# Low-rank token mixer after a Mamba-2 block: U's product as complete sums per channel tile, V's product as four 32-row matmuls

## The chip, the cores and the metric

The kernel runs on one core of a Trainium2 chip, everything in float32. The metric is the device time of one execution in microseconds (us). An execution under the profiler gives the profile that is quoted here.

## What is computed

Two stages follow each other. The first is a chunked state-space recurrence (Mamba-2) over 4 batches of 8 heads, 768 tokens, 32 channels per head; the second is a mixer over tokens of low rank and an MLP over channels. Cut to what matters for the change:

```python
def _moe_ref(x, U, V, w_ch1, w_ch2):          # x: (4, 768, 256), output of the first stage
    xt = x.transpose(0, 2, 1)                 # (4, 256, 768)
    h = xt @ U @ V                            # U: (768, 32), V: (32, 768)
    u = x + h.transpose(0, 2, 1)
    ch = np.maximum(u @ w_ch1, 0.0) @ w_ch2   # (256, 1024), (1024, 256)
    return (u + ch).astype(np.float32)
```

The weights U, V, w_ch1 and w_ch2 arrive as 64-bit floats and are made into 32-bit floats on the chip.

## The kernel before, in words

**Stages.** The program walks over 12 pairs of 128-token chunks (`pairs`, three for each batch). For pair k, `prep` scales B and C on VectorE and GpSimd, `turn` transposes them on TensorE (L298), `gram` multiplies them (L311, four groups of 32 rows, result in the PSUM tile `g` of four banks, masked into `M` by VectorE at L316), `state` carries the recurrence (L331, L345, L350), `ychannel` forms the output with channels on partitions (L368, L375, four groups of 32 columns; copied to `yT` by ScalarE at L378), and `ytokens` transposes it back (L386, copied to `ytok` by VectorE at L388).

**Mixer.** Once the three pairs of a batch are done, `mixer(b)` hands out its work in pieces that are spread between the steps of the next batch's pairs. `project` (L403) multiplies U with `ytok`: six matmuls, one for each token chunk, each giving 32 rows by 256 channels; chunk c goes to column group c % 4, so that the result holds four partial sums on 128 partitions, which ScalarE copies to `pT` (L405). Four pieces `mixed(k, n)` (L409) then multiply a 128-channel half of `pT` with `V4`, which holds V four times on 128 partitions: the product over 128 rows also adds up the four partial sums. VectorE adds the result to `uT` (L412). `up` (L419) is the first product of the MLP, with the relu on ScalarE (L424) or VectorE (L422), `down` (L431, L435) the second, copied out by ScalarE (L437).

**Weights.** `load_words` (L119) and the loop at L126 bring the 64-bit words into a ring of six buffers (`words`). `to_fp32` turns one buffer into 32-bit floats with five VectorE instructions (L237 `e`, L244 `top`, L241 `power`, L246 `top`, L248 `rest`), one on ScalarE (L240) and one on GpSimd (L250). There are eleven such pieces: U, V in two halves of 384 columns, four of w_ch1 and four of w_ch2. They are spread between the steps of the first batch.

**What sets the order.** The order on TensorE is the order of the program text, with the pieces dealt out by `some(n)` in the main loop: at a batch's end all that is left is issued, and then the first pieces of the new mixer. On the other engines and on the DMA queue (all loads are issued from SyncE, the row SP) a scheduler sets the order when the kernel is built. Each queue runs in that order, so that an instruction that waits holds up what is behind it.

Of the kernel before, what the change touches and what calls it, by code (L numbers as in the profile page):

```python
# [9 lines left out]
FP32 = mybir.dt.float32  # L10
# [5 lines left out]
ALU = mybir.AluOpType  # L16
# [4 lines left out]
def kernel(  # L21
# [27 lines left out]
    nc = tc.nc  # L49
    P = 128  # L50
    NB, NH, S, D = x.shape
    N = B.shape[-1]
    NC = S // P
    NPR = NC // 2
    DM = NH * D
    RK = moe_U.shape[1]
    DF = moe_w_ch1.shape[1]
    NM = DF // P
    NCB = DM // P
    HS = S // 2  # L60
    HT = HS // P
    Q = 32
    assert D == Q and 2 * N == Q and NH == 8 and RK == Q and NC % 2 == 0

    const = ctx.enter_context(tc.tile_pool(name="const", bufs=1))
    raw = ctx.enter_context(tc.tile_pool(name="raw", bufs=9))
    att = ctx.enter_context(tc.tile_pool(name="att", bufs=2))
    mix = ctx.enter_context(tc.tile_pool(name="mix", bufs=2))
# [5 lines left out]
    def bank(tag, *dims):  # L74
        return psum.tile([P, *dims], FP32, tag=tag, name=tag, bufs=BANKS[tag])
# [4 lines left out]
        out=a_sb,  # L80
        in_=a.rearrange("(g b) h (c s) -> g (b h c) s", g=2, s=P).rearrange(
            "g r s -> r g s"))
# [18 lines left out]


    U_sb = const.tile([P, NC, RK], FP32)
    V4 = const.tile([P, S], FP32)
    w1 = const.tile([P, NCB, DF], FP32)
    w2 = const.tile([P, NM, DM], FP32)
    weights = []
# [1 line left out]
    def words_of(dst):  # L109
        p, i, j = dst.shape  # L110
        t = raw.tile([P, 2 * WCOLS], INT32, tag="words", name="words", bufs=NWORDS)
        weights.append((dst, t[:p, :2 * i * j]))
        return t[:p, :2 * i * j]

    def load_words(dst, src):

        p, i, j = dst.shape
        t = words_of(dst)
        nc.sync.dma_start(out=t.rearrange("p (i j) -> p i j", i=i), in_=src)  # L119

    U2, V2, w12, w22 = (w.bitcast(INT32) for w in (moe_U, moe_V, moe_w_ch1, moe_w_ch2))
    load_words(U_sb, U2.rearrange("(c p) r -> p c r", p=P))
    for k in range(2):
        t = words_of(V4[:, None, ts(k, HS)])
        for g in range(4):
            nc.sync.dma_start(out=t[ts(g, RK)], in_=V2[:, ts(k, S)])  # L126
    for k in range(DF // WCOLS):
        for c in range(NCB):
            load_words(w1[:, c, None, ts(k, WCOLS)],
# [14 lines left out]
    def triangle(name, out, pattern, base, mult, in_=None):  # L144
# [9 lines left out]
           for v in range(2)]  # L154
# [7 lines left out]
                            op=ALU.subtract)  # L162
# [16 lines left out]
    for b in range(NB):  # L179
        g, o = divmod(b * NH * NC, R)  # L180
        nc.vector.tensor_scalar(
            out=la[:, b].rearrange("p c h -> p h c"),
            in0=la_ps[:, g, o:o + NH * NC].rearrange("p (h c) -> p h c", h=NH),
# [16 lines left out]
    for v in range(2):  # L200
# [14 lines left out]
        out=own, in0=d.rearrange("p b c (g r) -> p (b c g) r", r=4),  # L215
        in1=rmask[:, None, :].to_broadcast(own.shape), op=ALU.mult)
# [39 lines left out]
    for i in range(2):  # L256
        t = const.tile([P, 2 * NH, 2, N], FP32, name=f"bd{i}")
# [3 lines left out]
    yT, ytok = {}, {}  # L261
# [5 lines left out]
    def prep(k):  # L267
        b, q = pairs[k]
        bc = bc_sb.pop(k)
        s = st[k] = {}  # L270
        cs = slice(2 * q, 2 * q + 2)
        shape = [P, 2 * NH, 2, N]
        for i, (name, F, eng) in enumerate((("Bs", FB, nc.vector), ("Cs", FC, nc.gpsimd))):
            s[name] = t = att.tile(shape, FP32, tag=name, name=name)
            eng.tensor_tensor(  # L275
                out=t,
                in0=bc[:, i].rearrange("p c h n -> p (c h) n")[:, :, None, :].to_broadcast(shape),
                in1=F[:, b, cs].rearrange("p c h v -> p (c h) v")[:, :, :, None].to_broadcast(
                    shape),
                op=ALU.mult)  # L280
        s["bd"] = bd = bds[k % 2]
        n = 2 if q < NPR - 1 else 1
        sh = [P, n * NH, N]
        nc.gpsimd.tensor_tensor(
            out=bd[:, :n * NH, 0],
            in0=bc[:, 0, :n].rearrange("p c h n -> p (c h) n"),
            in1=FD[:, b, 2 * q:2 * q + n].rearrange("p c h -> p (c h)")[:, :, None].to_broadcast(
                sh),
            op=ALU.mult)

    def turn(k, c):

        s = st[k]
        tp = bank("w", 4, P)
        for i, name in enumerate(("Bs", "Cs")):
            flat = s[name].rearrange("p h v n -> p (h v n)")
            for g in range(2):
                nc.tensor.transpose(out=tp[:, 2 * i + g], in_=flat[:, ts(2 * c + g, P)],  # L298
                                    identity=ident)
        s["T", c] = T = att.tile([P, 4, P], FP32, tag="T", name="T", bufs=4)  # L300
        nc.scalar.copy(out=T, in_=tp)  # L301
# [91 lines left out]

    def mixer(b):
        uT = yT[b]
        pT = mix.tile([P, DM], FP32, tag="pT", name="pT")
        gT, hold = {}, {}

        def project():

            p = bank("w", DM)
            for c in range(NC):
                nc.tensor.matmul(out=p[ts(c % 4, Q)], lhsT=U_sb[:, c], rhs=ytok[b][:, c],  # L403
                                 start=(c < 4), stop=(c >= NC - 4), skip_group_check=True)
            nc.scalar.copy(out=pT, in_=p)  # L405

        def mixed(k, n):
            h = bank("w", HS)
            nc.tensor.matmul(out=h, lhsT=pT[:, ts(n, P)], rhs=V4[:, ts(k, HS)],  # L409
                             start=True, stop=True)  # L410
            u = uT[:, n, ts(k, HS)]
            nc.vector.tensor_tensor(out=u, in0=h, in1=u, op=ALU.add)  # L412

        def up(k, m):
            if m == 0:
                gT[k] = mix.tile([P, NM, HS], FP32, tag="gT", name="gT")
            g = bank("w", HS)
            for n in range(NCB):
                nc.tensor.matmul(out=g, lhsT=w1[:, n, ts(m, P)], rhs=uT[:, n, ts(k, HS)],  # L419
                                 start=(n == 0), stop=(n == NCB - 1))  # L420
            if m % 2:
                nc.vector.tensor_relu(gT[k][:, m], g)  # L422
            else:
                nc.scalar.activation(gT[k][:, m], g, AF.Relu)  # L424

        def down(k, j):
            if j == 0:
                hold[k] = mix.tile([P, HT, DM], FP32, tag="o", name="o")
            o = bank("w", DM)
            for n in range(NCB):  # L430
                nc.tensor.matmul(out=o[:, ts(n, P)], lhsT=uT[:, n, ts(HT * k + j, P)], rhs=ident,  # L431
                                 is_transpose=True, start=(n == 0), stop=False,
                                 skip_group_check=True)
            for m in range(NM):
                nc.tensor.matmul(out=o, lhsT=gT[k][:, m, ts(j, P)], rhs=w2[:, m],  # L435
                                 start=False, stop=(m == NM - 1), skip_group_check=True)
            nc.scalar.copy(out=hold[k][:, j], in_=o)  # L437
            if j == HT - 1:
                nc.sync.dma_start(
                    out=out[b, ts(k, HS)].rearrange("(j p) m -> p j m", p=P),  # L440
                    in_=hold[k])

        pieces = [project]
        for k in range(2):
            for n in range(NCB):
                pieces.append(lambda k=k, n=n: mixed(k, n))
        for k in range(2):
            for m in range(NM):
                pieces.append(lambda k=k, m=m: up(k, m))
            for j in range(HT):  # L450
                pieces.append(lambda k=k, j=j: down(k, j))
        return pieces


    with tc.manual_schedule(engines={PE}):
        last = len(pairs)
        prep(0)
        turn(0, 0)
        turn(0, 1)
        state(0)  # L460
        gram(0)
        prep(1)
        pieces = [lambda w=w: to_fp32(*w) for w in weights]
        for k in range(last + 1):
            b, q = divmod(k, NPR)

            def some(n):
                for _ in range(min(n, len(pieces))):
                    pieces.pop(0)()

            if k:
                ytokens(k - 1)
            if q == 0 and b:
                some(len(pieces))
                pieces = mixer(b - 1)
                some(5)
            if k == last:
                break
            quota = -(-len(pieces) // (NPR - q))
            parts = [quota // 3, quota // 3, quota - 2 * (quota // 3)]  # L480
            if k + 2 < last:
                prep(k + 2)
            if k + 1 < last:
                turn(k + 1, 0)
                some(parts[0])
                turn(k + 1, 1)
            else:
                some(parts[0])
            some(parts[1])
            ychannel(k)  # L490
            if k + 1 < last:
                state(k + 1)
                gram(k + 1)
            some(parts[2])
        some(len(pieces))
# [30 lines left out]
```

## Time and profile before

| what | us |
|---|---|
| median of 3 runs | 303.73 (302.91 to 304.68) |
| the profiled execution, its own time | 303.6 |
| its span, first to last instruction | 301.9 |
| busy in it: TensorE matmul (PE) | 258.4 |
| TensorE weight load (PEld) | 194.6 |
| VectorE (DVE) | 113.8 |
| ScalarE (ACT) | 58.5 |
| GpSimd (POOL) | 53.2 |

The profile's page gives busy time and idle time of each engine, a strip of 40 slices of the span, and the chain of waits that ended last. The trace behind it gives single instructions in order of time. A float32 matmul of the program appears as two matmul records there, so that a count of x8 is four matmuls of the program. SPq is the instruction queue of SyncE, from which the loads are issued.

### The profile page before, as it was taken

The numbers are of one execution on the slowest core, as the hardware profiler recorded it, in microseconds if no ns is written. First come the engines' busy times: TensorE is split into PE (matmuls) and PEld (weight loads), VectorE is DVE, ScalarE is ACT, GpSimd is POOL, SyncE is SP. The second block draws the span as 40 slices with busy tenths as digits, with TensorE's granted clock in tenths as the row PEclk, the third lists the DMA queues.
The fourth block names the chain that finished last, engine by engine and source line by source line (L and its number), as shares of the span: only waits on it lengthen the run. The fifth ranks groups of instructions, "written<-read, shape, count | busy, mean of one in ns | idle before, by whom it ended". The sixth has DMA issues, their size and how long they took to land.

```text
span 301.9 us, 4870 instructions
## 1 busy us (share of the span) xinstructions
PE 258.4 (86%) x2094; PEld 194.6 (64%) x2094; DVE 113.8 (38%) x201; ACT 58.5 (19%) x115; POOL 53.2 (18%) x69
## 2 busy tenths in 40 slices
PE   4549409019999999999999999999999999999994
PEld 4438307005768868857688688566886785587583
DVE  3249999994350154032500541325005103200200
ACT  5112213101221121013212220022121101111100
POOL 4343357461301103002102040001000000000000
PEclk9755967756999999999999999999999999999999
DMA  7989399899820100010001000100010001001001
GB/s 90 101 185 318 110 185 111 105 108 110 93 33 0 54 1 2 0 52 2 0 2 54 0 3 0 52 2 2 0 52 2 2 0 52 0 2 52 0 0 52
DMA packets 81141, 15.02 MB, mean 50 GB/s; under 512 B 76064, under 2 KB 79328, under 8 KB 81120
## 3 DMA queue, kind: packets, MB, share of 16 engines
q1 hardware_dynamic: 81120, 14.72, 27.5%
q8 instruction: 16, 0.26, 0.4%
q14 instruction: 5, 0.04, 0.0%
HBM read 11.57 MB, written 3.15 MB: 49 GB/s over the span
## 4 chain that ended last, share of the span: by engine, by line
PE 77%; DVE 10%; SPq 5%; DMA 3%; issue 1%; POOL 1%; ACT 1%; DVEq 0%; POOLq 0%
PE w L419 28%; PE w L435 27%; PE w L409 5%; PE y L375 4%; PE g L311 3%; PE y L368 3%; PE w L298 2%; SPq L93 2%; DVE M L316 2%; PE w L431 2%; DMA words<-in_moe_U_dram 2%; DVE rest L248 2%; SPq L94 2%; SPq L97 1%; DVE top L244 1%
## 5 line engine op out<-in xcount | busy, mean ns | idle before, releaser
L419 PE MATMUL w<-yT,w 128*128 128x384 f32 x256 | 86.9, 489 | 0.0
L435 PE MATMUL w<-w,gT 128*128 128x256 f32 x384 | 86.9, 379 | 0.0
L435 PEld LDWEIGHTS w<-w,gT 128*128 128x128 f32 x384 | 71.1, 190 | 8.7
L419 PEld LDWEIGHTS w<-yT,w 128*128 128x128 f32 x256 | 47.3, 190 | 29.3
L422 DVE TENSOR_SCALAR gT<-w 128x384 f32<-128x384 f32 x32 | 17.8, 557 | 64.0 <-PE w L419 64.0
L275 POOL TENSOR_TENSOR Cs<-bc,FC 128x512 f32<-128x512 f32 x12 | 16.4, 1364 | 78.5 <-issue 46.1
L316 DVE TENSOR_TENSOR M<-g,causal 128x1024 int32<-128x1024 int32 x24 | 28.3, 1217 | 3.1 <-PE g L311 3.0
L424 ACT ACTIVATE gT<-w 128x384 f32<-128x384 f32 x32 | 15.7, 491 | 55.3 <-PE w L419 55.3
L437 ACT COPY o<-w 128x256 f32<-128x256 f32 x24 | 8.9, 372 | 82.5 <-PE w L435 82.5
L301 ACT COPY T<-w 128x512 f32<-128x512 f32 x24 | 13.7, 585 | 36.8 <-PE w L298 36.4
L350 POOL TENSOR_TENSOR wide<-S,rmask 128x256 f32<-128x256 f32 x20 | 12.4, 633 | 47.4 <-DVE S L345 47.3
L388 DVE COPY ytok<-w 128x512 f32<-128x512 f32 x12 | 8.2, 683 | 31.4 <-PE w L386 31.4
L275 DVE TENSOR_TENSOR Bs<-bc,FB 128x512 f32<-128x512 f32 x12 | 10.8, 897 | 23.7 <-PE w L298 14.6
L345 DVE SCALAR_TENSOR_TENSOR S<-S,kept,w 128x32 f32<-128x32 f32 x32 | 6.3, 243 | 32.1 <-PE w L331 17.0
L375 PE MATMUL y<-M,x 128*32 128x128 f32 x384 | 14.4, 289 | 4.6 <-DVE M L316 4.6
L298 PE MATMUL w<-ident,Bs 128*128 128x128 f32 x48 | 10.6, 307 | 9.0 <-DVE Bs L275 9.0
L403 PE MATMUL w<-ytok,U_sb 128*32 128x256 f32 x48 | 5.5, 411 | 14.5 <-DVE ytok L388 14.5
L311 PE MATMUL g<-T 32*128 32x128 f32 x384 | 15.9, 308 | 0.0
L409 PE MATMUL w<-V,pT 128*128 128x384 f32 x32 | 13.9, 585 | 1.9 <-ACT pT L405 1.9
L298 PEld LDWEIGHTS w<-ident,Bs 128*128 128x128 f32 x48 | 7.1, 161 | 12.9 <-DVE Bs L275 9.0
L375 PEld LDWEIGHTS y<-M,x 128*32 128x32 f32 x384 | 10.2, 114 | 7.2 <-DVE M L316 5.9
L368 PEld LDWEIGHTS y<-T,wide 128*128 128x128 f32 x80 | 11.8, 212 | 4.3 <-POOL wide L350 1.9
(68 smaller groups left out, 195.3 us busy)
## 6 DMA issues: line engine op xcount, KB each, us to landing
words<-in_moe_w_ch_dram SPq DMA_DIRECT2D x8, 512.0 KB, 4.5
x<-in_x_dram SPq DMA_DIRECT2D x24, 128.0 KB, 3.8
out_dram<-o SPq DMA_DIRECT2D x8, 384.0 KB, 2.5
bc<-in_B_dram SPq DMA_DIRECT2D x24, 64.0 KB, 3.8
bc<-in_C_dram SPq DMA_DIRECT2D x24, 64.0 KB, 3.6
words<-in_moe_V_dram SPq DMA_DIRECT2D x8, 96.0 KB, 2.3
words<-in_moe_U_dram SPq DMA_DIRECT2D x1, 192.0 KB, 4.9
a_sb<-in_a_dram SPq DMA_DIRECT2D x1, 96.0 KB, 2.0
```

Of the source, the lines that this page charges most:

```text
L275: eng.tensor_tensor(out=t, in0=bc[:, i].rearrange("p c h n -> p (c h) n")[:, :, None, :].to_broadcast(shape), in1=F[:, b, cs].rearrange("p ...
L298: nc.tensor.transpose(out=tp[:, 2 * i + g], in_=flat[:, ts(2 * c + g, P)], identity=ident)
L301: nc.scalar.copy(out=T, in_=tp)
L311: nc.tensor.matmul(out=g_ps[:, r, c, g], lhsT=T[rows, g], rhs=T[rows, 2 + g], start=True, stop=True, skip_group_check=True)
L316: nc.vector.tensor_tensor(out=M[:, :, c].bitcast(INT32), in0=g_ps[:, :, c].bitcast(INT32), in1=causal[:, None, None, :].to_broadcast(sh), ...
L368: nc.tensor.matmul(out=y[:, c, g], lhsT=wide[:, g].rearrange("p r d -> p (r d)"), rhs=s["T", c][:, 2 + g], start=fresh, stop=False, skip_g ...
L375: nc.tensor.matmul(out=y[ts(r, Q), c, g], lhsT=x_sb[k][:, c, 4 * g + r], rhs=s["M"][:, r, c, g], start=False, stop=True, skip_group_check= ...
L409: nc.tensor.matmul(out=h, lhsT=pT[:, ts(n, P)], rhs=V4[:, ts(k, HS)], start=True, stop=True)
L419: nc.tensor.matmul(out=g, lhsT=w1[:, n, ts(m, P)], rhs=uT[:, n, ts(k, HS)], start=(n == 0), stop=(n == NCB - 1))
L422: nc.vector.tensor_relu(gT[k][:, m], g)
L424: nc.scalar.activation(gT[k][:, m], g, AF.Relu)
L435: nc.tensor.matmul(out=o, lhsT=gT[k][:, m, ts(j, P)], rhs=w2[:, m], start=False, stop=(m == NM - 1), skip_group_check=True)
```

## The change

`project` now issues 24 matmuls: for each of the six chunks four of 32 rows by 128 channels, one into each column group q. Group q multiplies channel tile q // 2, and a group's six matmuls accumulate, so that each group of 32 partitions of `pT` holds a complete sum (each channel tile twice). `V4` holds V's column half q % 2 in partition group q, half as wide as before. `mixed` is one piece: four matmuls over 32 rows each, in four row groups, into the four banks of the PSUM tile `g`; then the four additions in the order 0, 2, 1, 3. V is loaded with four transfers in place of eight and made into 32-bit floats by one `to_fp32` piece in place of two.

```diff
-    V4 = const.tile([P, S], FP32)
+    V4 = const.tile([P, HS], FP32)
...
-    for k in range(2):
-        t = words_of(V4[:, None, ts(k, HS)])
-        for g in range(4):
-            nc.sync.dma_start(out=t[ts(g, RK)], in_=V2[:, ts(k, S)])
+    t = words_of(V4[:, None])
+    for q in range(4):
+        nc.sync.dma_start(out=t[ts(q, RK)], in_=V2[:, ts(q % 2, S)])
...
-        pT = mix.tile([P, DM], FP32, tag="pT", name="pT")
+        pT = mix.tile([P, P], FP32, tag="pT", name="pT")
...
-            p = bank("w", DM)
+            p = bank("w", P)
             for c in range(NC):
-                nc.tensor.matmul(out=p[ts(c % 4, Q)], lhsT=U_sb[:, c], rhs=ytok[b][:, c],
-                                 start=(c < 4), stop=(c >= NC - 4), skip_group_check=True)
+                for q in range(4):
+                    nc.tensor.matmul(out=p[ts(q, Q)], lhsT=U_sb[:, c],
+                                     rhs=ytok[b][:, c, ts(q // 2, P)],
+                                     start=(c == 0), stop=(c == NC - 1), skip_group_check=True)
             nc.scalar.copy(out=pT, in_=p)
 
-        def mixed(k, n):
-            h = bank("w", HS)
-            nc.tensor.matmul(out=h, lhsT=pT[:, ts(n, P)], rhs=V4[:, ts(k, HS)],
-                             start=True, stop=True)
-            u = uT[:, n, ts(k, HS)]
-            nc.vector.tensor_tensor(out=u, in0=h, in1=u, op=ALU.add)
+        def mixed():
+
+            h = bank("g", 4, 4 * P)
+            for q in range(4):
+                rows = ts(q, Q)
+                nc.tensor.matmul(out=h[:, q, :HS], lhsT=pT[rows], rhs=V4[rows],
+                                 start=True, stop=True, skip_group_check=True)
+            for q in (0, 2, 1, 3):
+                u = uT[:, q // 2, ts(q % 2, HS)]
+                nc.vector.tensor_tensor(out=u, in0=h[:, q, :HS], in1=u, op=ALU.add)
...
-        pieces = [project]
-        for k in range(2):
-            for n in range(NCB):
-                pieces.append(lambda k=k, n=n: mixed(k, n))
+        pieces = [project, mixed]
...
-                some(5)
+                some(2)
```

On TensorE, at the end of each batch, the queue held this before (here the second batch; `L298` is `turn`, `L419` is `up`):

```order
L386 MATMUL w<-ident,yT 128x128 x4
L403 MATMUL w<-ytok,U_sb 32x256 x6
L409 MATMUL w<-V_97,pT 128x384 x4
L298 MATMUL w<-ident,Bs 128x128 x2
L298 MATMUL w<-ident,Cs 128x128 x2
L419 MATMUL w<-yT,w_98 128x384 x4
```

and holds this now, from `project` on, with the waits that the instructions carry:

```order
L403 MATMUL w<-ytok,U_sb 32x128 [waits Activation_49]
L403 MATMUL w<-ytok,U_sb 32x128 x15
L403 MATMUL w<-ytok,U_sb 32x128 [waits DVE_49]
L403 MATMUL w<-ytok,U_sb 32x128 x7
L413 MATMUL g<-V_97,pT 128x384 [waits Activation_49]
L413 MATMUL g<-V_97,pT 128x384 x3
L297 MATMUL w<-ident,Bs 128x128 [waits PE_49]
L297 MATMUL w<-ident,Bs 128x128
L297 MATMUL w<-ident,Cs 128x128 x2
L424 MATMUL w<-yT,w_98 128x384 [waits DVE_49] x2
```

The place is the same; `project` has four times as many matmuls, the four of V's product stand without a wait between them, and the first two matmuls of `up` (over the two channel tiles) each carry a wait of their own on VectorE.

On VectorE, while the weights are made into 32-bit floats, this stood before (128x384 are the halves of V, 128x512 is the first piece of w_ch1):

```order
L237 TENSOR_SCALAR e<-words 128x384
L244 TENSOR_SCALAR top<-words 128x384
L241 SCALAR_TENSOR_TENSOR power<-words,power 128x384
L237 TENSOR_SCALAR e<-words 128x512
L316 TENSOR_TENSOR M<-g,causal 128x4x256 x2
L246 TENSOR_TENSOR top<-top,power 128x384
L248 SCALAR_TENSOR_TENSOR rest<-words,power 128x384
L241 SCALAR_TENSOR_TENSOR power<-words,power 128x512
```

and now, from the first instruction of V on:

```order
L236 TENSOR_SCALAR e<-words 128x384
L243 TENSOR_SCALAR top<-words 128x384
L236 TENSOR_SCALAR e<-words 128x512
L243 TENSOR_SCALAR top<-words 128x512
L240 SCALAR_TENSOR_TENSOR power<-words,power 128x384
L344 SCALAR_TENSOR_TENSOR S<-S,kept,w 128x32
L245 TENSOR_TENSOR top<-top,power 128x384
L247 SCALAR_TENSOR_TENSOR rest<-words,power 128x384
```

The second half of V is gone (the rows before are those of that half), and two instructions of w_ch1's first piece have moved up between V's `top` and V's `power`.

On SyncE's queue the loads of weights and of the next pair (`bc`, `x`) stood so before:

```order
L119 DMA words<-in_moe_U_dram 128x6x64
L126 DMA words<-in_moe_V_dram 32x768 x8
L119 DMA words<-in_moe_w_ch_dram 128x1024 x4
L119 DMA words<-in_moe_w_ch_dram 128x2x512 x3
L93 DMA bc<-in_B_dram 128x8x16
```

and stand so now:

```order
L119 DMA words<-in_moe_U_dram 128x6x64
L125 DMA words<-in_moe_V_dram 32x768 x4
L119 DMA words<-in_moe_w_ch_dram 128x1024 x4
L119 DMA words<-in_moe_w_ch_dram 128x2x512 x2
L93 DMA bc<-in_B_dram 128x8x16
```

Four transfers of V fewer stand ahead of the next pair's loads, and one transfer of w_ch2 fewer, which now comes behind them.

## Rows read from the trace of the kernel before

**Rows 1.** The page: span, and the strip of 40 slices (tenths of each slice).
```profile
span 301.9 us, 4870 instructions
...
PE   4549409019999999999999999999999999999994
...
DVE  3249999994350154032500541325005103200200
...
PEclk9755967756999999999999999999999999999999
```
**Rows 2.** Windows: length, busy us (instructions) of PE, PEld, DVE, ACT, POOL; clock, DMA share, GB/s.
```profile
53.00:66.90 13.90, 0.10 (x4) 0.00 (x0) 13.90 (x22) 2.17 (x3) 8.31 (x7) 0.62 0.94 104
66.90:73.40 6.50, 5.95 (x12) 2.94 (x13) 4.10 (x8) 0.37 (x1) 1.26 (x1) 0.50 1.06 113
73.40:80.00 6.60, 6.60 (x28) 4.17 (x27) 1.81 (x4) 2.15 (x4) 1.54 (x1) 0.99 1.04 113
```
**Rows 3.** The chain that ended last, around the first batch's end: start, us, what.
```profile
66.33 0.61 DVE ytok L388
...
66.98 1.09 PE w L403 x4
...
68.52 5.31 PE w L409 x8
73.83 0.44 PE w L298 x4
74.26 1.94 PE w L419 x6
```
**Rows 4.** The timeline of VectorE, GpSimd and SP's queue while V is made into floats.
```profile
23.99 0.35 DVE L237 TENSOR_SCALAR e<-words 128x384 int32<-128x384 int32 x1
...
25.02 0.56 DVE L241 SCALAR_TENSOR_TENSOR power<-words,power 128x384 int32<-128x384 int32 x1 [0.41 <-ACT power L240]
...
27.28 0.90 DVE L237 TENSOR_SCALAR e<-words 128x384 int32<-128x384 int32 x1
...
29.67 0.41 DVE L237 TENSOR_SCALAR e<-words 128x512 int32<-128x512 int32 x1
...
32.27 0.54 DVE L246 TENSOR_TENSOR top<-top,power 128x384 int32<-128x384 int32 x1
...
33.21 0.68 DVE L241 SCALAR_TENSOR_TENSOR power<-words,power 128x512 int32<-128x512 int32 x1
33.81 1.22 DVE L244 TENSOR_SCALAR top<-words 128x512 int32<-128x512 int32 x1
...
33.36 1.38 POOL L250 TENSOR_TENSOR V<-rest,top 128x384 f32<-128x384 f32 x1 [4.03 <-DVE rest L248]
...
20.78 15.24 SPq L119 DMA_DIRECT2D words<-in_moe_w_ch_dram  x7
```
**Rows 5.** The timeline around the second batch's end, all engines.
```profile
130.25 0.64 PE L403 MATMUL w<-ytok,U_sb 128*32 128x256 f32 x8
...
131.77 0.37 ACT L405 COPY pT<-w 128x256 f32<-128x256 f32 x1 [1.48 <-PE w L403]
...
132.20 2.85 PE L409 MATMUL w<-V,pT 128*128 128x384 f32 x8 [0.47 <-ACT pT L405]
133.15 1.20 DVE L412 TENSOR_TENSOR yT<-w,yT 128x384 f32<-128x384 f32 x2 [2.10 <-PE w L409]
```
**Rows 6.** The same timeline, the products in column groups (L375) and row groups (L311).
```profile
141.46 1.08 PE L375 MATMUL y<-M,x 128*32 128x128 f32 x32
...
142.61 0.59 ACT L378 COPY yT<-y 128x512 f32<-128x512 f32 x1 [2.28 <-PE y L375]
142.76 1.17 PE L311 MATMUL g<-T 32*128 32x128 f32 x32
...
144.00 2.36 DVE L316 TENSOR_TENSOR M<-g,causal 128x1024 int32<-128x1024 int32 x2 [0.29 <-PE g L311]
```
**Rows 7.** The chain that ended last, at the last batch's end.
```profile
252.33 2.85 PE w L409 x8
```

## The prediction, made before the change had run

> **What bounds the kernel now.** I read the page's strip first. From about 75 us on TensorE is busy without a break and its granted clock is full; before that VectorE is the busy engine, TensorE mostly waits, and the clock is often near half [rows 1]. The kernel has two regimes, then: up to the first batch's end VectorE makes the weights into floats, after it TensorE streams the MLP. The windows show where one passes into the other: from 53.0 to 66.9 us VectorE is busy for all 13.90 us and TensorE for 0.10; from 66.9 to 73.4 TensorE is busy for 5.95 of 6.50 us, at a clock of 0.50, the lower level of 1.2 GHz; then the clock is full [rows 2]. The chain says the same in single steps: VectorE's copy of the last tokens at 66.33, U's product from 66.98, V's product from 68.52 for 5.31 us, `turn` for 0.44, and `up` from 74.26 [rows 3]. So three things can move the end: VectorE's work before 66.3, the steps between that copy and the first `up` of each of the four batches, and the time at which the clock rises.
>
> The sum is made against the profiled execution's own 303.6 us, which is 0.13 under the median of the runs, 303.73. About 0.5%, or 1.5 us, is what a measurement of this kernel can tell from no change.
>
> **The change part by part.**
>
> *One conversion fewer.* VectorE's five instructions for V's second half stood on the chain. From the start of its `e` at 27.28 to the next piece's `e` at 29.67 are 2.39 us, from its second `top` at 32.27 to the next piece's `power` at 33.21 are 0.94 us [rows 4]: 3.33 us. Some of it was not the instructions' own: undisturbed, `e` takes 0.35 and `power` 0.56 [rows 4], and two of the first length and three of the second make 2.4 us; the rest came while GpSimd worked beside them, and GpSimd's work for the first half stays. On the other side GpSimd's addition for the second half (33.36, 1.38 us) goes, beside which a `top` of w_ch1 took 1.22 us where `e` of the same shape takes 0.41 [rows 4]: 0.8 more. And the 0.41 us for which `power` waited for ScalarE [rows 4] is now filled by two instructions of w_ch1. The bounds are 2.0 us (the five overlap a little at their ends) and 4.5 us (3.33 + 0.8 + 0.41). I take 2.4 + 0.8, less the overlap: **3.1 us**. The work queued behind is VectorE's own, so the saving should reach the copy at 66.33. ScalarE's and GpSimd's instruction for that half go too; both had slack (2.17 and 8.31 us busy of 13.90, [rows 2]), and I give nothing for them.
>
> *Loads.* Four transfers fewer stand ahead of w_ch1, and the next pair's loads stand before a load of w_ch2 that waited for a free buffer: in the row of 15.24 us, seven issues of weights held up everything behind them [rows 4]. VectorE was busy anyway in that time, so earlier data brings nothing by itself: 0 us. What could cost is that VectorE now needs w_ch1's first piece two places after V; its load is issued four transfers earlier, which is my reason to expect no wait.
>
> *U's product, full clock (second to fourth batch).* It becomes 24 matmuls of 128 columns, six in each column group. The rate: `up` takes 1.94 us for three matmuls of 384 columns [rows 3], 0.647 each, 1.68 ns a column. The nearest rows are `ychannel`'s, 16 matmuls of the same shape in four column groups: from their start at 141.46 to ScalarE's copy at 142.61 are 1.15 us [rows 6], against 4 x 128 x 1.68 ns = 0.86 us of streaming in one group, so that 0.29 us is start and tail. Six in a group: 1.29 + 0.29 = 1.58 us. Sixteen of the 24 need only older tokens and run while VectorE copies the last ones. Before, U's product began at 130.25 and the copy to `pT` at 131.77 [rows 5]; now that copy would begin at 131.83. It has 128 columns: 256 take 0.37 us [rows 5] and 512 take 0.59 [rows 6], so about 0.26. V's product then begins at 132.15 (0.06 for the two signals), as before (132.20).
>
> *V's product, full clock.* Before: 2.85 us from 132.20, then `turn` for 0.44, so `up` began at 135.49 [rows 3, 5]. Now four matmuls run side by side. The nearest rows are `gram`'s: 16 matmuls over 32 rows in four row groups and four banks, 142.76 to VectorE's first mask at 144.00, 1.24 us, of which 0.86 is streaming [rows 6]. One matmul of 384 columns in each group streams 0.647, so the first addition can begin 1.03 us after the start, at 133.18. An addition takes about 0.56 (two in 1.20 with a wait between, [rows 5]); `turn` lies beside it. `up` begins with the tile that the first addition makes, at 133.8, and its second matmul wants the second addition, which is done before the first matmul's 0.647 us are over. Gain 1.7 us each at the second and third batch: **3.4 us**. At the fourth there is no `turn`: before, `up` began at 252.33 + 2.85 = 255.18 [rows 7]; now 1.6 us after a start at 252.3, at 253.9. Gain **1.2 us**. The other two additions run beside `up`; the banks of `g` are next wanted by `gram`, some ten us later.
>
> *A rule that speaks against it.* The rows of `gram` hold 0.38 us over streaming, with products of another shape on both sides [rows 6], and the sum has this once for each batch. The Trainium skill, "TensorEngine Tiling (Array Packing)", section Key Properties, says that a change of tiling mode drains the engine; the change adds one such switch for each batch. If the overhead of `gram`'s rows did not hold that drain, a second 0.38 us would come on top four times, and the sum would be 1.5 us later.
>
> *The first batch's end, at half clock.* The copy begins at 66.33 - 3.1 = 63.2, and TensorE goes on at 63.9 (66.98 less 3.1). Eight matmuls of U's product are left: 1.2 us at half clock, ScalarE's copy and signals 0.3, so V's product begins at 65.4. Its first addition begins 1.03 + 0.65 = 1.7 us later, at 67.1, and `up` could begin at 67.7; but `turn` behind V's product, 0.9 us at this clock, ends at 67.9. `up` begins at 67.9 instead of 74.26: 6.3 us earlier, of which 3.1 is the conversion.
>
> But at 74.26 the clock was full. It rose at 73.4 [rows 2], 4.9 us after V's product had begun and 6.4 us after TensorE had resumed. If it again rises 4.9 us after V's product begins, that is 70.3; from 67.9 to 70.3 `up` runs at half speed and loses 1.2 us. Bounds: no loss, if it rises as `up` begins; 3.2 us, if only the unbroken work counts and it takes the 6.4 us from there. I take 1.2, the row's own distance. Net **5.1 us**.
>
> Sum: 5.1 + 3.4 + 1.2 = 9.7; 303.6 - 9.7 = **293.9 us**.
>
> **The rivals.**
>
> *The conversion saves nothing.* VectorE then waits for data where V's second half was: for w_ch1's first piece, or for the next pair. For it: the DMA share is 0.94 to 1.06 around 66.9 us [rows 2]. Against it: VectorE never waited for those transfers before, and there are fewer bytes. The first `up` is then at 71.0; V's product begins at 68.5 as before, so the clock rises at 73.4 and 1.2 us are lost. The first batch's end brings 2.0 instead of 5.1: 297.0 us.
>
> *The additions become the bound.* `up` waits for all four. The Trainium skill, the same page, section PSUM Bottleneck, warns that tiling speeds up TensorE and not the emptying of PSUM. The mechanism here: V's product takes a quarter of the streaming time, and the additions keep their 0.56 us. If all four had to be done, `up` would begin about 1.5 us later at each batch: 1.5 x 3, and 1.1 at the first (partly at half clock), 5.6 in all: 299.5 us. Against it: the first two matmuls of `up` each have a wait of their own on VectorE.
>
> *The clock falls at the later batch ends.* TensorE now idles around 0.3 us for `pT` and 0.2 to 1 for the first addition. Each fall would cost half of a stretch as long as the 6.4 us above, 3.2 us, three times 9.6: 303.5 us, no change. Against it: before, it stood idle for 0.47 us at the same place [rows 5] and the strip stays at 9 [rows 1].
>
> *Slower: the column groups do not run side by side in U's product.* All four read the same tokens through separate weights. One after another, 24 matmuls of 0.215 us are 5.2 us instead of 1.58: 3.6 more at three batch ends, and 2.3 at the first, where eight are left at half clock; 13.1 in all, 307.0 us. It decides from about 4.0 us for the 24 on, where the loss is the gain. Against it: `ychannel`'s 16 take 1.08 us [rows 6], and eight records before, 0.64 us [rows 5], were four matmuls of 0.43 us each, already side by side.
>
> **How the numbers follow.** Forecast 0.78, first rival 0.10, additions 0.05, clock 0.04, column groups 0.03. Only the last two are not faster by over 0.5%; half a hundredth or so of the forecast goes there too. Faster 0.92, same 0.04, slower 0.04. The range: from 293.9 the conversion's upper bound takes 1.4 off and the clock's 1.2; both at once are unlikely, 291.6. Upwards the conversion's lower bound adds 1.1, the clock's 2.0, the second drain 1.5; the first rival lies at 297.0. Two of these at once, or the first rival with one, give about 298.2. Beyond it lie the last three rivals, 0.12, and a little of the forecast.
>
> **What would show it.** In the profile after: the copy to `ytok` before U's product near 63.2; TensorE's first `up` near 67.9 and the clock's rise near 70.3; U's product in 1.6 us and V's in about 1.0 at the later batches; `up` 1.6 us after V's product begins. The prediction is wrong if VectorE shows idle time on a DMA before 60 us, if `up` follows the fourth addition, or if the clock leaves its full level after 80 us.

## The result, and the profile after

| | before | changed |
|---|---|---|
| median, us | 303.83 (302.91 to 304.68, 4 runs) | 295.37 (294.73 to 296.49, 4 runs) |
| the profiled execution's own time, us | 303.6 | 296.49 |
| its span, us | 301.9 | 294.8 |

The ratio is 0.9726, with a 95% interval of 0.9683 to 0.9769: 2.7% faster, 1.5 us slower than the 293.9 us of the forecast and inside its range. The profiled execution of the changed kernel was the slowest of its four, so that its trace shows a gain of 7.1 us where the medians show 8.5.

The page of the changed kernel, the lines that answer to [rows 1]:

```profile
span 294.8 us, 5144 instructions
...
PE   4447631819999999999999999999999998999994
...
DVE  2339999794530244034401541325005103200100
...
PEclk9776955775999999999999999999999999999999
```

The two regimes are still there, VectorE first and TensorE after, and the clock never leaves its full level once it has risen. The first batch's end in the chain that ended last (start, us, what), for [rows 3]:

```profile
64.69 0.61 DVE ytok L387
...
65.35 1.13 PE w L403 x16
...
66.82 1.66 PE g L413 x8
68.48 1.05 PE w L297 x4
69.53 4.02 PE w L424 x8
```

The copy stands 1.64 us earlier than before, not 3.1. From there to the first `up` (L424) are 4.84 us, where it had been 7.93 and 4.7 were forecast. Eight records of `up` take 4.02 us, which is neither the 2.58 of the full clock nor twice that. The windows show why, for [rows 2]:

```profile
65.30:72.20 6.90, 6.47 (x33) 3.66 (x34) 4.35 (x8) 0.92 (x3) 1.27 (x1) 0.50 0.90 95
72.20:80.00 7.80, 7.80 (x118) 5.65 (x118) 2.98 (x8) 2.08 (x4) 3.11 (x4) 0.99 1.09 118
```

The clock stays at 0.50 (1.2 of 2.4 GHz) until 72.3, so `up` ran for 2.77 us at half speed, and its eight records took 1.44 us longer than 2.58 (1.2 forecast). At the second batch's end the timeline of all engines reads, for [rows 5]:

```profile
126.96 1.52 PE L403 MATMUL w<-ytok,U_sb 128*32 128x128 f32 x48
...
128.54 0.27 ACT L406 COPY pT<-w 128x128 f32<-128x128 f32 x1 [1.54 <-PE w L403]
...
128.86 0.93 PE L413 MATMUL g<-V,pT 32*128 32x384 f32 x8 [0.39 <-ACT pT L406]
...
129.92 1.95 DVE L417 TENSOR_TENSOR yT<-g,yT 128x384 f32<-128x384 f32 x4 [2.17 <-PE g L413]
...
130.54 0.30 PEld L424 LDWEIGHTS w<-yT,w 128*128 128x128 f32 x2 [0.40 <-DVE yT L417]
130.54 2.85 PE L424 MATMUL w<-yT,w 128*128 128x384 f32 x8 [0.17 <-DVE yT L417]
131.00 1.77 PEld L424 LDWEIGHTS w<-yT,w 128*128 128x128 f32 x6 [0.17 <-DVE yT L417]
```

U's product takes 1.58 us up to ScalarE's copy (1.58 forecast), V's product 1.06 up to the first addition (1.03), and `up` begins 1.68 us after V's product (1.65). But its first eight records take 2.85 us instead of 2.58. Three narrow windows of TensorE's timeline, each of which takes in one record more, show where the 0.27 us lie:

```profile
130.54 0.59 PE L424 MATMUL w<-yT,w 128*128 128x384 f32 x1 [0.17 <-DVE yT L417]
...
130.54 0.91 PE L424 MATMUL w<-yT,w 128*128 128x384 f32 x2 [0.17 <-DVE yT L417]
...
130.54 1.24 PE L424 MATMUL w<-yT,w 128*128 128x384 f32 x3 [0.17 <-DVE yT L417]
```

The first record takes 0.59 us, and each further one adds 0.32 or 0.33, as in an unbroken row of them (2.58 for eight). The third belongs to the second matmul; the load of its weights waited for the second addition and began at 131.00, but it came in time. So the 0.27 us are all the first record's: its weight load waits for the first addition together with the matmul and begins only at 130.54, where there is no matmul left in front to hide it. V's product of the kernel before took the same 2.85 for eight records of 384 columns, after one wait [rows 5]. That is 0.27 us at each of the three later batches; at the first, `turn` stands right in front of `up`.

### The profile page after: what moved, and what is told of

The parts are those of the page before. It is cut to its first block, busy times and chain, and to the rows that moved or that the text cites. A ratio compares the mean times of both kernels' runs of the same rounds, so it can differ in the third digit from the quotient of the medians.

```text
span 294.8 us, 5144 instructions
## 1 busy us (share of the span) xinstructions
PE 252.9 (86%) x2238; PEld 193.3 (66%) x2238; DVE 109.2 (37%) x196; ACT 57.1 (19%) x114; POOL 50.9 (17%) x68
## 4 chain that ended last, share of the span: by engine, by line
PE 77%; DVE 9%; SPq 7%; DMA 3%; issue 1%; POOL 1%; ACT 1%; DVEq 0%; POOLq 0%
PE w L424 29%; PE w L440 28%; PE y L374 4%; PE g L310 3%; PE y L367 3%; SPq L94 3%; SPq L93 2%; DVE M L315 2%; PE w L297 2%; DMA words<-in_moe_U_dram 2%; SPq L97 2%; PE w L436 2%; PE w L403 2%; DVE rest L247 2%; PE g L413 2%; DVE power L240 1%
## 5 line engine op out<-in xcount | busy, mean ns | idle before, releaser
L424 PE MATMUL w<-yT,w 128*128 128x384 f32 x256 | 88.7, 497 | 1.1 <-DVE yT L417 1.1
L424 PEld LDWEIGHTS w<-yT,w 128*128 128x128 f32 x256 | 48.0, 193 | 32.0 <-DVE yT L417 2.7
L274 POOL TENSOR_TENSOR Cs<-bc,FC 128x512 f32<-128x512 f32 x12 | 15.5, 1290 | 74.8 <-issue 44.7
L374 PE MATMUL y<-M,x 128*32 128x128 f32 x384 | 15.1, 300 | 6.7 <-DVE M L315 6.7
L367 PE MATMUL y<-T,wide 128*128 128x128 f32 x80 | 12.1, 294 | 7.4 <-POOL wide L349 7.2
L274 DVE TENSOR_TENSOR Bs<-bc,FB 128x512 f32<-128x512 f32 x12 | 9.3, 776 | 23.6 <-PE w L297 14.6
L249 POOL TENSOR_TENSOR w<-rest,top 128x512 f32<-128x512 f32 x8 | 12.1, 1508 | 16.0 <-DVE rest L247 15.4
L310 PEld LDWEIGHTS g<-T 32*128 32x128 f32 x384 | 13.6, 212 | 0.6
```

The costliest lines, as they stand in the source:

```text
L274: eng.tensor_tensor(out=t, in0=bc[:, i].rearrange("p c h n -> p (c h) n")[:, :, None, :].to_broadcast(shape), in1=F[:, b, cs].rearrange("p ...
L310: nc.tensor.matmul(out=g_ps[:, r, c, g], lhsT=T[rows, g], rhs=T[rows, 2 + g], start=True, stop=True, skip_group_check=True)
L367: nc.tensor.matmul(out=y[:, c, g], lhsT=wide[:, g].rearrange("p r d -> p (r d)"), rhs=s["T", c][:, 2 + g], start=fresh, stop=False, skip_g ...
L374: nc.tensor.matmul(out=y[ts(r, Q), c, g], lhsT=x_sb[k][:, c, 4 * g + r], rhs=s["M"][:, r, c, g], start=False, stop=True, skip_group_check= ...
```

## The experiments

They ran in two groups, each on one chip together with the kernel before. Its median was 304.1 us in the group of the repetition, the products, the conversion and the filler, and 303.99 in the group of the other four. The changed kernel's 295.82 us, which the others are held against, is of the first group.

### The changed kernel again

No edit.

> The changed kernel once more, unchanged, as the level that the others are compared with and for a second profile. Expected 295.4 us (294.7 to 296.5). What the second profile should settle: in the first one U's words landed 0.84 us later than before the change (20.48 against 19.64). If that comes from w_ch1's loads standing four transfers earlier, they land late again, near 20.4; if it is a thing of one execution, they land near 19.7 and the copy to ytok stands near 63.9 instead of 64.69.

Measured: 295.82 us (294.88 to 296.23), ratio 0.9741 (0.9694 to 0.9788). U's words did land earlier this time, by 1.19 us, but the copy stood at 64.30, only 0.39 earlier, since VectorE then waited in another place. Its timeline:

```profile
19.31 0.26 DVE L236 TENSOR_SCALAR e<-words 128x192 int32<-128x192 int32 x1 [2.99 <-DMA words<-in_moe_U_dram]
25.00 0.43 DVE L236 TENSOR_SCALAR e<-words 128x512 int32<-128x512 int32 x1 [0.74 <-DMA words<-in_moe_w_ch_dram]
55.81 0.43 DVE L243 TENSOR_SCALAR top<-words 128x512 int32<-128x512 int32 x1 [1.61 <-POOL w L249]
```

So the late landing of U is no property of the change: in ten profiled executions of these kernels VectorE began U's `e` between 18.98 and 20.50 us. The second row is the wait that the first rival named, for w_ch1's first piece, 0.74 us long, in one execution of the eight that have that order. It is also one of the signs of being wrong that the prediction named, idle time of VectorE on a DMA before 60 us. But the first row is such a time too, and the kernel before has it as well (3.26 us, for U's words), so that this sign could not decide anything. The third row is in both profiles of the changed kernel and was not in that of before: 1.6 us.

### The products alone

```diff
+    V5 = const.tile([P, HS], FP32)
+    t = words_of(V5[:, None])
+    for q in range(4):
+        nc.sync.dma_start(out=t[ts(q, RK)], in_=V2[:, ts(1 - q % 2, S)])
```

> The changed kernel with a second V buffer loaded and made into floats that nothing reads, so that the loads and conversions of the first batch stand as before the change. Theory (the gain has two parts, and the conversion is one): only the products' gain is left, by the first profile 3.1 at the first batch's end less 1.3 for the clock, 1.4 at the second and third and 0.95 at the fourth, 5.5 in all: 298.3 us, with the copy to ytok before U's product near 66.3 again. Rival (the conversion saves nothing): 295.4, as the changed kernel.

Measured: 298.07 us (297.03 to 298.5), ratio 0.9814 (0.9766 to 0.9863). The copy is back at 66.36, and VectorE never waits for GpSimd's addition:

```profile
66.36 0.61 DVE ytok L391
...
68.48 1.66 PE g L417 x8
70.14 1.05 PE w L301 x4
71.19 2.83 PE w L428 x8
```

The products bring 6.0 us of the gain, the loads and the conversion the rest: 295.82 against 298.07. The rival that the conversion saves nothing is out.

### The conversion alone

```diff
-    V4 = const.tile([P, S], FP32)
+    V4 = const.tile([P, HS], FP32)
...
-    for k in range(2):
-        t = words_of(V4[:, None, ts(k, HS)])
+    for k in range(1):
+        t = words_of(V4[:, None])
...
-            nc.tensor.matmul(out=h, lhsT=pT[:, ts(n, P)], rhs=V4[:, ts(k, HS)],
+            nc.tensor.matmul(out=h, lhsT=pT[:, ts(n, P)], rhs=V4,
```

> The kernel before the change with V's second half neither loaded nor converted; both halves of the tokens are multiplied with V's first half, so that part of the computation is left out (V's second half) while the products keep their number and size. Theory: the copy to ytok comes 1.6 to 3.3 us earlier, and the end with it: 300.5 to 302.2 us; the sum of this gain and that of products_only is the whole gain of 8.4. Rival (the conversion saves nothing): 303.8. A third reading: the two gains do not add, since the clock's rise takes back a part when both are there; then their sum is above 8.4.

Measured: 300.6 us (299.27 to 301.99, 10 runs), ratio 0.9908 (0.9879 to 0.9937), 3.5 us or 0.9%. The copy comes at 63.43, 2.9 us before the 66.33 of [rows 3]; 0.3 of that is U's landing. Even so VectorE waits for GpSimd:

```profile
54.95 0.43 DVE L244 TENSOR_SCALAR top<-words 128x512 int32<-128x512 int32 x1 [1.53 <-POOL w L250]
```

The two gains alone, 6.0 and 3.5, make 9.5, and together they are 8.3. With intervals of about a half per cent each (1.5 us), the difference of 1.2 is not resolved, and whether they add is left open.

### Three buffers for the conversion's temporaries

```diff
-            t = att.tile([P, WCOLS], dtype, tag=name, name=name)
+            t = att.tile([P, WCOLS], dtype, tag=name, name=name,
+                         bufs=3 if name in ("top", "rest") else 2)
```

> The changed kernel with three buffers instead of two for the temporaries top and rest of the conversion; the order on every engine stays the same. It tests the stall of 1.6 us that VectorE has at 54.6 in the changed kernel and did not have before: a top waits for GpSimd's addition of two pieces earlier, which stands behind a multiplication that waits for TensorE. Theory (that stall took back part of the conversion's gain): it goes, the copy to ytok comes 1.6 us earlier, and the end by 0.8 to 1.6 us, as the clock's rise follows or not: 294.0 to 295.0 us against 295.6. Rival (VectorE then waits as long at the next place, for data or for GpSimd): the copy stays near 64.5, 295.6 us.

Measured: 295.7 us (295.05 to 296.9, 6 runs), ratio 0.973 (0.9704 to 0.9756). The theory fell and the rival held. The wait for GpSimd is gone, and in its place stands this, on VectorE and ScalarE, with GpSimd's addition:

```profile
55.16 2.05 DVE L241 SCALAR_TENSOR_TENSOR power<-words,power 128x512 int32<-128x512 int32 x2 [0.59 <-ACT power L240]
```

```profile
53.92 0.58 ACT L378 COPY yT<-y 128x512 f32<-128x512 f32 x1 [5.18 <-PE y L375]
54.40 1.33 ACT L240 ACTIVATE power<-e,bias 128x512 int32<-128x512 int32 x2
```

```profile
54.79 1.27 POOL L250 TENSOR_TENSOR w<-rest,top 128x512 f32<-128x512 f32 x1
```

ScalarE's part of the conversion stands behind its copy of `yT`, which waits for TensorE; so VectorE waits 0.59 us, and its two `power` then take 2.05 us, with GpSimd's addition beside them, where they took 1.29 in the changed kernel, after that addition. Both waits go back to one place in the changed kernel's order. The timelines of its TensorE, GpSimd and VectorE:

```profile
50.27 2.08 PE L367 MATMUL y<-T,wide 128*128 128x128 f32 x8 [6.48 <-POOL wide L349]
...
53.98 0.66 PE L330 MATMUL w<-x,bd 128*32 128x32 f32 x32
```

```profile
49.42 0.80 POOL L349 TENSOR_TENSOR wide<-S,rmask 128x256 f32<-128x256 f32 x1
...
54.54 0.40 POOL L283 TENSOR_TENSOR bd<-bc,FD 128x128 f32<-128x128 f32 x1 [3.31 <-PE w L330]
54.90 1.28 POOL L249 TENSOR_TENSOR w<-rest,top 128x512 f32<-128x512 f32 x1
```

```profile
56.55 1.29 DVE L240 SCALAR_TENSOR_TENSOR power<-words,power 128x512 int32<-128x512 int32 x2
```

GpSimd's `wide` comes late in its queue, TensorE stands still for 6.48 us for it, GpSimd's `bd` waits 3.31 us for TensorE, and the conversion's addition is behind `bd`. The three-buffer kernel shows that more buffers for the temporaries don't help; whether an earlier `wide` would was not tried.

### Filler matmuls that keep the clock up

```diff
+FILL = 11
...
+                if b == 0 and c == 3:
+                    f = bank("y", 4, P)
+                    for _ in range(FILL):
+                        nc.tensor.matmul(out=f[:, :3], lhsT=w1[:, 0, :P], rhs=uT[:, 0, :HS],
+                                         start=True, stop=True, skip_group_check=True)
```

> The changed kernel with eleven more matmuls of 384 columns between the 16th and the 17th matmul of the first batch's U product, into a PSUM tile that nobody reads; they fill the 7.7 us in which TensorE waits for VectorE's copy. Theory (the low clock costs time there): the clock is still full when the copy lands, U's last eight matmuls take 0.55 us instead of 1.15, V's product 1.0 instead of 1.66, the first up begins near 68.3 (VectorE's conversion of the last weights, until 67.7, now holds the additions) instead of 69.5 and runs at full speed: 2.5 us less, 292.9 us. Rival (the clock's cost is hidden behind VectorE's own work): 295.4. If the filler ends too late, TensorE resumes later than 65.35 and the time is above 295.4.

Measured: 292.97 us (292.49 to 293.43), ratio 0.9651 (0.9606 to 0.9696); 292.9 was expected. TensorE's timeline and the windows:

```profile
56.49 7.36 PE L410 MATMUL y<-yT,w 128*128 128x384 f32 x22
64.33 0.64 PE L404 MATMUL w<-ytok,U_sb 128*32 128x128 f32 x16 [0.47 <-DVE ytok L388]
65.36 0.93 PE L419 MATMUL g<-V,pT 32*128 32x384 f32 x8 [0.39 <-ACT pT L412]
...
67.20 2.85 PE L430 MATMUL w<-yT,w 128*128 128x384 f32 x8 [0.33 <-DVE yT L423]
```

```profile
54.00:64.30 10.30, 9.86 (x90) 6.10 (x86) 8.77 (x17) 2.17 (x4) 6.44 (x6) 1.00 0.81 92
64.30:67.20 2.90, 2.16 (x28) 1.11 (x29) 2.90 (x6) 0.50 (x2) 0.44 (x1) 1.00 1.01 127
```

The clock is full throughout. V's product takes 0.93 us where it took 1.66, and `up` begins 3.5 us after the copy's start (63.67) instead of 4.84, and at full speed. From the copy's start to the end of the first eight records of `up` are 6.4 us where the changed kernel's first profile has 8.9: there the low clock cost 2.5 us, the size that was expected. The medians differ by 2.85 (295.82 to 292.97); the rest is less than what the time up to the copy differs by between executions without the filler. The four runs lie within 0.94 us, but the five of the kernel with all three edits, whose clock is full there too, within 1.41, and the changed kernel's within 1.35: that the clock's rise is what makes runs differ is not shown.

### The additions in plain order

```diff
-            for q in (0, 2, 1, 3):
+            for q in range(4):
```

> The changed kernel with the four additions in the order 0, 1, 2, 3 instead of 0, 2, 1, 3, so that the second matmul of the first up needs the third addition and not the second. Theory (after V's product TensorE waits for the additions, one at a time as it needs them): the second matmul starts 0.46 us later at each of the three later batches and some 0.3 at the first, 1.4 to 1.7 us in all, 297.0 to 297.3 against 295.6. Rival (up waits for all four anyway): no change. In the trace the first up's matmul starts 1.68 us after V's product in both.

Measured: 295.13 us (294.62 to 296.33, 6 runs), ratio 0.9713 (0.9688 to 0.9738): no difference from the changed kernel that can be measured, where 1.4 to 1.7 us were expected. The trace shows the mechanism, and a smaller price:

```profile
129.54 0.91 PE w L424 x2
130.45 0.02 issue
130.47 2.20 PE w L424 x6
```

The second matmul now waits for the third addition, which is done as the first matmul ends, so that TensorE loses only 0.02 us by the wait itself. But its weight load now begins with no matmul in front to hide it, as the first one's does: two records take 0.91 us, which are two of 0.32 and 0.27, and six take 2.20, six of 0.32 and 0.27 again. The eight take 3.13 us with the 0.02 instead of 2.85: 0.28 us at each later batch, not 0.46. Three times 0.28 is 0.8 us, too little to be seen where the six runs lie 1.7 us apart.

### Both turns ahead of the first up

```diff
                 turn(k + 1, 0)
+                if q == 0 and b:
+                    turn(k + 1, 1)
                 some(parts[0])
-                turn(k + 1, 1)
+                if not (q == 0 and b):
+                    turn(k + 1, 1)
```

> The changed kernel with both turns of the next pair ahead of the first up at the ends of the first three batches, so that TensorE has 0.44 us more to do while VectorE makes the first two additions. Theory: the first up loses its wait of 0.17 us and the 0.27 us by which its second matmul came late (its weight load stands behind the wait for the second addition): 0.4 us each at the second and third batch, nothing at the first, where TensorE's turn already outlasts the addition: 294.8 against 295.6, which a measurement cannot tell from no change; the trace can (eight records of up in 2.58 us after V's product instead of 2.85). Rival (the load of the second matmul's weights is late for another reason): 2.85 again.

Measured: 293.61 us (292.51 to 295.35, 4 runs), ratio 0.9675 (0.9641 to 0.971). The chain at the second batch's end:

```profile
126.68 1.02 PE w L297 x8
127.70 5.16 PE w L424 x16
```

and TensorE's weight loads there:

```profile
127.43 0.30 PEld L424 LDWEIGHTS w<-yT,w 128*128 128x128 f32 x2
127.89 3.07 PEld L424 LDWEIGHTS w<-yT,w 128*128 128x128 f32 x10 [0.16 <-DVE yT L417]
```

Sixteen records in 5.16 us are 2.58 for eight: the time came out as the theory has it, and TensorE waits no more. The theory's reason did not: the load of the second matmul's weights still waits for the second addition (the second row, 0.16 us), and nothing is lost by it. What the edit removes is the first matmul's wait, so that its weight load (the first row) runs behind `turn` again. That accounts for 0.4 us each at the second and third batch. The rest of the 2 us to the changed kernel is not shown to be the edit's; in the profiled execution U's words were there early (`e` at 18.98), and the clock had risen at 68.1, before `up` began at 68.31, which belong to that execution.

### All three together

Nine filler matmuls, three buffers, both turns first.

> The changed kernel with filler matmuls (nine, as the gap is shorter), three buffers and both turns first. If the three add up: 292.97 less 1.5 less 0.8, 290.7 us. If the copy to ytok does not come earlier with three buffers, 292.3.

Measured: 291.97 us (291.39 to 292.8, 5 runs), ratio 0.9604 (0.9581 to 0.9628), near the 292.3 that was expected if the buffers bring nothing. It is the fastest version: 3.4 us under the changed kernel's first median of 295.37, most of it from the filler.

## Why the prediction was right, and where its sizes were off

**Right.** Both regimes, both parts of the gain and their places. The steps at the later batches came as worked out: U's product 1.58 us, V's product 1.06 to the first addition, `up` 1.68 us after its start, and at the fourth batch's end 5.17 us from the start of `ytokens` to `up` became 3.95, a gain of 1.2. U's column groups run side by side (24 matmuls in 1.49 us on the chain), so the slower rival is out; the clock stays full after its rise, so that rival is out as well.

**The sum of the trace.** At the first batch's end `up` began 4.73 us earlier (74.26 to 69.53) and lost 1.44 by the clock: 3.3. At the second and third 1.65 less 0.27, 1.4 each. At the fourth 1.22 less 0.27, 0.95. Together 7.0, where the two profiled executions differ by 7.1 (303.6 to 296.49). The forecast had 9.7. The ends of its range do not follow from its terms to the tenth (the two downward ones make 291.3, not 291.6; two upward ones 296.5 to 297.4), but the result lies well inside by either count.

**Right in size, not in its reasons: the conversion, 3.1 us.** In the first profile it brought 1.64 at the copy; U's late landing took 0.84, by chance. From U's `e` to the copy's start the executions show:

| kernel | U's `e` | copy | between |
|---|---|---|---|
| before | 19.66 | 66.33 | 46.7 |
| products alone | 19.06 | 66.36 | 47.3 |
| changed, first and second profile | 20.50, 19.31 | 64.69, 64.30 | 44.2, 45.0 |
| conversion alone | 19.32 | 63.43 | 44.1 |
| additions in order, three buffers | 20.48, 20.15 | 64.09, 64.07 | 43.6, 43.9 |
| filler, both turns, all three | 20.04, 18.98, 19.08 | 63.67, 62.69, 63.03 | 43.6, 43.7, 44.0 |

The two executions that convert V's second half take 46.7 and 47.3 us, the eight that don't 43.6 to 45.0, in the mean 3.0 less; by the medians the step brings 2.25 us (products alone against the changed kernel) and 3.5 (conversion alone). So the size holds, with about a microsecond between executions. In the first profile the step is worth 2.5: VectorE's idle time in it rose from 0.6 us to 1.6, and the rest fell by 3.5. What failed is the sentence that gave nothing for GpSimd's and ScalarE's instructions because both had slack over 13.90 us: the queues stood in another order, and VectorE waited 1.6 us for one of them at 54.6. That this wait took anything from the gain is not shown, since without it the three-buffer kernel is no faster. Of the first rival's mechanism, a wait for data, one execution shows 0.74 us; the 1.6 us are a wait for GpSimd, and stand far behind the place where V's second half was converted.

**Off: a term that was missing.** The sum let the second addition finish beside the first matmul of `up`, and so it does. But it let `up` stream from its first moment on, at 0.647 us a matmul, though it comes out of a wait, and then the first weight load is not hidden: 0.27 us three times, 0.8 in all. The price stood in the rows: V's product before took 2.85 us [rows 5] where four times 0.647 are 2.59. The rival of the additions is out: `up` follows the first of them. Of the section PSUM Bottleneck of the Trainium skill's page "TensorEngine Tiling (Array Packing)" the trace bears out this much: the first addition stands on the path with 0.57 us, the other three do not.

**Right in kind, chance in size: the clock, 1.2 us.** It was 1.44 in the first profile. The rise came 6.5 us after TensorE resumed in the kernel before, and with the changed products, without the filler, 6.9 and 6.7 (changed), 6.2 (additions in order), 4.8 (both turns), 4.7 (three buffers) and 4.6 us (products alone) after. What the first eight records of `up` lose by it went from 0 to 1.44 us over these executions, and no run shows what decides it.

**The drain.** The rule of the Trainium skill, same page, section Key Properties, that a change of tiling mode drains the engine, was priced at a second 0.38 us for each batch if `gram`'s rows did not hold it. V's product took 1.06 us up to the first addition where 1.03 with one such overhead was forecast, so a second one does not show on the path. TensorE stands idle for 0.39 us in front of it, and whether a drain lies in there cannot be seen.

## What to carry to other kernels

A stretch in which one engine works off a queue and the others seem to have slack is costed with the order that the new kernel has: read which instruction of the slack engine stands behind a wait, and who waits for it. Where TensorE stands idle before a chain of dependent steps, look at the clock of these steps; idle time can be filled with matmuls that nobody reads, which here brought another 2.85 us. And an operand that comes late holds up the weight load of its matmul too, even when the weights were there long before: behind another matmul that costs nothing, after a wait of TensorE it cost 0.27 us here.

## What the runs showed of the hardware

- Products over 32 rows in four row groups, float32, 384 columns each: four matmuls with all their starts and ends took 0.97 us on the chain at the full clock and 1.66 at half; the four of 128 rows that they replace took 2.85 and 5.31 (during which the clock rose).
- The time from TensorE's resumption at the first batch's end to the clock's rise differs from execution to execution of nearly the same program: 4.6 to 6.9 us, with the changed kernel itself at 6.9 and 6.7.
- The first of a row of matmul records of 384 columns took 0.59 us after a wait, and each one after it added 0.32, at the full clock (changed, additions in order). With other matmuls right in front the first added 0.32 as well, though the next matmul's weight load was held up by 0.16 us (both turns).
- The same pair of VectorE's `power` took 2.05 us with GpSimd's addition beside it (three buffers) and 1.29 after it (changed).
